# Gates, second shift and second scale as rows on four column tiles, carried to columns through DRAM

## The chip, the cores and the metric

The kernel runs on one core of one Trainium2 chip. The metric is the device time of one execution in microseconds, the median over runs. TensorE (PE in the profile; its weight loads are PEld), VectorE (DVE), ScalarE (ACT) and GpSimd (POOL) compute, and SyncE (SP) issues nearly all DMAs here. Each engine works through its own list of instructions in order.

## The reference

One transformer block on x of 2048 rows and 448 columns (S, D), in bf16, with six modulation vectors made from a row c:

```
mod = silu(c) @ w_mod                      # 448 -> 6 x 448
sa, ca, ga, sb, cb, gb = the six vectors of 448
h = layernorm(x) * (1 + ca) + sa
x = x + ga * A(h)                          # A: attention, 16 heads of 28, causal, window 256, then @ wo
h = layernorm(x) * (1 + cb) + sb
x = x + gb * B(h)                          # B: gated MLP with a spatial matmul
B(h): z = gelu(h @ w_in)                   # 448 -> 1792
      z1 = z[:, :896];  z2 = layernorm(z[:, 896:])
      g = w_sp @ z2 + b_sp                 # w_sp is 2048 x 2048
      return (z1 * g) @ w_out              # 896 -> 448
```

sa and sb are shifts, ca and cb scales, ga and gb gates.

## The kernel before, in words

**Tiles.** The 2048 rows are 16 tiles of 128 (NT) in four blocks of 512 (NB4). D is cut into four chunks of the contraction (DC; the last chunk has 64 rows of real data and is padded). An activation is kept transposed as hT, features on partitions and rows on the free axis, whenever it feeds a matmul as an operand over features.

**Order of the work.** Every instruction, or small group of them, is registered with `add` as an operation with its dependencies, the engines it may go to, and a duration for each. A planner has written a string ORDER (L19 to L75): one word `number.engine.slots` for each operation in the order of emission. `Sched.order` walks the string, puts every operation at the end of its engine's list and takes buffers by the slots; `count`, `waits` and `emit` then put in the semaphores. The durations and the constants beside them (HOP, NEXT, PEL, the `lat` and `tail` of a DMA) only feed the planner; what the program does is set by ORDER and the dependencies. An engine that waits holds everything behind it in its list.

**Stages, as the profile shows them.** Up to about 15 us: loads, the first modulation (t_mA, L554 to L564, in columns on PE), layer norm of the first block, its transposes on PE (L708), and warm matmuls on the identity (L578) that fill PE. About 15 to 110 us: projections to q, k, v (L756, L798, L840) and attention. A unit is a tile j of queries and half of the heads: scores on PE (L968, four row tiles of 32; L977 for some of the blocks, through QBD, which q_load copies from qT with four DMAs, L666), exponentials on ACT (L929), masks on DVE (L984), P times V on PE (L1011), then reciprocal and scaling on DVE (L1025, L1027). A DMA transpose (L476) turns o_sb into hT, PE multiplies by wo_g (L1035) and DVE adds to x (L1040). The second layer norm follows (`stats` L618, `norm` L638: DVE, POOL or ACT, L641 to L650), a DMA transpose, and the second modulation on hT (L1058 on ACT or L1060 on DVE or POOL). About 108 to 154 us: the two halves of w_in (L1097, L1143) with gelu on ACT, layer norm of z2 on POOL and DVE, ended by L1112 on POOL. From 154 us: 28 groups of 16 spatial matmuls (L1166), each of which depends on all z2 tiles, an addition on DVE (L1170), the product with z1 on POOL (L1173), the output projection (L1185), the residual on DVE (L1195) and the output DMA (L1200).

**The lines around the change.** After t_mA come, with scale and shift of the second modulation as columns, t_mB: 32 matmuls of one column each (L544, made by `mod_cols`), copied to modT by two DVE operations (`mod_out`, L569 and L570; the second adds 1), and a small DMA (d_modB, L589) that moves 64 partitions of modT up. t_gate (L591) makes the gates ga and gb as rows, broadcast on 64 partitions each: the stationary operand is sc_rep, silu(c) repeated in 64 columns, so that two column tiles hold the two gates. t_graw (L595) copies PSUM to gg_sb, and three DMAs (`spread`, L601) make both gates stand on all 128 partitions. POOL multiplies wo by ga (t_wog, L605, four operations) and w_out by gb (L1051, seven).

Of the kernel before, what the change touches and what calls it, by code (L numbers as in the profile page):

```python
# [9 lines left out]
HOP = 0.12  # L10

NEXT = {"dve": 0.08, "act": 0.11, "pool": 0.045}
# [11 lines left out]
187.p 188.p 189.p 193.p 179.p 192.p 181.a 182.a 150.v 151.v.2 197.v 157.a.3 183.a 167.p.5 164.p.6 191.p 218.p.3 190.p 168.v 169.a 195.a 165.v 166.v
194.v 200.p.7 226.v 230.v 227.v 219.a 180.a 196.a 204.a 201.p.5 198.p.6 202.v 232.v 231.v 228.v 229.v 233.v 53.v 205.a 199.p.1 203.a 378.p.0 209.p.0
220.p.7 224.p.6 206.p.1 379.a.0 384.p.0 225.a 44.g 51.g 213.v 52.v 43.g 234.g 235.g 210.a 385.a.1 207.p.0 211.a 221.a 380.v 382.v 236.v 239.g.0
237.v.1 113.p.1 238.v.2 115.v 240.v.3 114.v 403.p.0 117.p.0 388.v 118.v 244.p.1 208.p.6 404.a.2 405.a 212.a 245.v 386.v 241.p.0 410.p.0 222.p.7
381.p.0 383.p 214.s 217.s 216.s 215.s 17.s 24.s 20.s 18.s 22.s 120.s 119.s 21.s 19.s 246.a 242.v 243.v 411.a.3 249.p.1 223.a 412.a 250.a 247.p.0 248.a
430.p.0 432.p.0 387.p 389.p 431.a.4.0 275.v 279.v 281.v 277.v 282.v 280.v 278.v 276.v 283.g 326.v 284.g 390.v 391.v.0 285.v 332.v 413.v 406.v 408.v
287.v.0 415.v 434.v 288.g.1 292.s 291.s 253.p.1 261.p.0 254.a 438.p.0 262.a 439.a.5.1 265.p.1 407.p.0 259.p.0 409.p 266.a 260.a 459.p.0 460.a.6.2  # L30
433.a 251.p.1 414.p 267.p.0 416.p 467.p.0 468.a.0.3 328.v 289.v.2 293.s 286.v.3 330.v 252.v 435.v 290.s 268.v 417.v 418.v.1 329.v 263.p.1 440.p.0
273.p.0 441.a 264.a 257.s 256.s 121.s 258.s 255.s 392.s 419.s 436.p.0 488.p.0 464.v 333.v 327.v 331.v 442.v 443.v 489.a.1.4 437.p 444.p 271.p.1
461.p.0 445.p 463.v 334.g 471.v 274.v 446.v 447.v.2 272.v 462.a 296.a 294.g 297.g 295.g 335.g 496.p.0 497.a.2.0 269.p.0 469.p.0 465.p.0 466.p 298.p.1
470.a 517.p.0 299.a 270.v 336.v 493.v 500.v 490.p.0 300.p.0 473.p 316.p.1 472.v 492.v 301.v 518.a.3.1 521.v 317.v 491.a 525.p.0 498.p.0 474.p
526.a.4.2 475.v 476.v.0 530.v 340.v.0 529.v 501.v 522.v 124.g 337.g.1 125.g 339.g.2 122.g 338.g.3 123.g 448.s 341.s 343.s 342.s 477.s 344.s 318.p.0
312.p.1 494.p.0 319.a 313.a 499.a 546.p.0 302.p.0 519.p.0 495.p 420.p.1 502.p 547.a.5.3 554.p.0 520.a 555.a.6.4 303.v 551.v 421.v 503.p 527.p.0
304.p.0 310.p.1 504.v 505.v.1 559.v 558.v 422.v 305.a 528.a 575.p.0 576.a.0.0 393.p.0 548.p.0 523.p.0 524.p 531.p 532.p 583.p.0 394.v 550.v 345.v
533.v 580.v 534.v.2 549.a 311.a 584.a.1.1 314.p.0 315.v 478.p.1 556.p.0 552.p.0 479.v 346.v 116.s 306.s 506.s 309.s 307.s 535.s 308.s 557.a 604.p.0
449.p.0 553.p 560.p 561.p 577.p.0 605.a.2.2 578.a 612.p.0 613.a.3.3 423.v 588.v 587.v 579.v 450.v 562.v 507.p.1 585.p.0 480.v 395.v 563.v.0 508.v
347.g 348.g 324.p.0 581.p.0 325.a 586.a 633.p.0 634.a.4.4 351.p.1 606.p.0 320.p.0 582.p 607.a 321.a 641.p.0 642.a.5.0 608.v 509.v 609.v 396.v 451.v  # L40
452.v 481.v 397.g 453.g 398.g 482.g 454.g 510.v 617.v 424.v 352.v 589.p 590.p 614.p.0 591.v 536.p.0 616.v 322.p.1 537.v 592.v.1 646.v 511.v 399.v
637.v 400.v.0 401.g 455.g 425.g 615.a 323.a 662.p.0 663.a.6.1 355.p.0 610.p.0 635.p.0 611.p 618.p 619.p 636.a 356.v 670.p.0 671.a.0.2 538.v 620.v
638.v 621.v.2 349.p.1 643.p.0 353.p.0 639.p.0 644.a 350.a 691.p.0 564.s 402.s 666.v 645.v 675.v 622.s 593.s 692.a.1.3 664.p.0 640.p 647.p 648.p
361.p.1 699.p.0 456.v.1 354.v 649.v 667.v 539.v 358.s 359.s 360.s 23.s 357.s 665.a 565.p.0 672.p.0 426.g 483.g 427.g.2 540.g 541.g 362.a 365.p.1
700.a.2.4 650.v.0 457.v 696.v 668.p.0 674.v 566.v 366.v 567.v 673.a 720.p.0 721.a.3.0 669.p 363.p.0 676.p 693.p.0 677.p 594.p.1 694.a 701.p.0 702.a
728.p.0 729.a.4.1 704.v 703.v 364.v 678.v 695.v 679.v.2 595.v 623.p.0 725.v 624.v 568.v 724.v 596.v 722.p.0 697.p.0 373.p.1 723.a 749.p.0 698.p 705.p
369.p.0 706.p 730.p.0 750.a.5.2 370.a 731.a 757.p.0 569.v 733.v 374.v 484.g 485.g.0 486.g 512.g 651.s 458.s 487.s 680.s 860.s 570.g 428.g 513.g 429.s
514.g.1 597.v 625.v 598.g 515.g 707.v 571.v 708.v.1 709.s 758.a.6.3 367.p.1 751.p.0 726.p.0 727.p 368.a 752.a 626.v 732.v 734.p 735.p 753.v 754.v
736.v 737.v.0 761.v 778.p.0 779.a.0.4 371.p.0 652.p.1 759.p.0 755.p.0 762.v 653.v 782.v 783.v 654.v 372.a 760.a 786.p.0 756.p 763.p 780.p.0 764.p
787.a.1.0 375.p.1 681.p.0 781.a 788.p.0 376.a 789.a 807.p.0 765.v 655.v 766.v.2 790.v 791.v 682.v 656.v 683.v 843.v 844.v 784.p.0 785.p 792.p 793.p  # L50
809.p.0 710.p.1 808.a.2.1 810.a 815.p.0 572.g.0 542.g 794.v 795.v.1 811.v 812.v 573.g 627.g 599.g 845.g 600.g 543.g.2 544.g 846.g 628.g 574.s 601.g.0
516.s 738.s 545.s 602.g 657.g 739.p.0 817.p.0 813.p.0 814.p 658.v 629.v 630.g.1 631.g 711.v 816.a.3.2 892.p.0 893.p.1 818.a 659.v.2 819.v 820.v 767.s
603.s 850.a 848.a 847.a 821.p 822.p 768.p.1 377.s 796.s 632.s 684.v 712.v 660.v 661.s 849.v 823.v 713.v 824.v.0 685.v 740.v 769.v 686.g 687.g 714.g
715.g 894.p 895.p 927.p.2 928.p.3 929.p 930.p 896.a 904.a 910.p.0 911.p.1 825.s 688.v.0 689.v 770.v 741.v 771.v 690.s 716.v 717.v.1 718.g 905.g 772.g
773.g 939.a 742.v 774.v 940.v 775.v.2 797.p.0 798.v 799.v 800.v 743.g 776.g 744.g 931.a 941.a.0 826.p.1 942.g 745.g 746.g.0 747.g 827.v 801.v 898.v
# [212 lines left out]
def bass_adaLN_cond__sliding_block__mixer_gmlp__prompt_kernel(  # L268
# [1000 lines left out]
```

## Time and profile before

| what | us |
|---|---|
| median of three runs | 276.64 |
| lowest and highest run | 275.81, 276.93 |
| profiled execution | 277.14 |
| its span, first to last instruction | 275.2 |
| PE busy in the span | 264.7 |
| DVE, ACT, POOL busy | 159.3, 138.2, 117.6 |

The granted clock of TensorE is 0.999 over the span. In the profile a line of a group reads: line of the kernel, engine, operation, output and inputs with their shapes, xcount, then the busy time in us and the mean of one in ns, then the idle time of the engine just before them and what ended it. A window reads: start and end, length, then the busy time and count of PE, PEld, DVE, ACT and POOL, the granted clock, the DMA share and GB/s. A piece of the chain reads: start, length, engine and line. Mean durations of matmuls overlap, as they are pipelined: 32 of 163 ns each are busy for 0.9 us together.

### The profile page before, as it was taken

The page shows a single profiled execution, that of the slowest core. Times are in us where ns is not written, and L with a number is a line of the kernel's source. Part 1 is how long each engine was busy: PE and PEld are TensorE (multiplying, and loading weights), DVE is VectorE, ACT ScalarE, POOL GpSimd, SP SyncE. Part 2 cuts the span into 40 slices and gives each one's busy share as a digit, 9 for nine tenths or more (in the row PEclk, how much of TensorE's full clock was granted, in tenths as well). Part 3 has the DMA queues.
Part 4 walks back from the last instruction along what each step waited for, and adds up shares of the span by engine and source line. Part 5 has one row for each costly group of instructions (what it writes and reads, how often), then busy time and mean ns, then how long its engine had stood idle before and what let it go on. Part 6 is the DMA issues. An engine that isn't in the chain of part 4 may idle for free.

```text
span 275.2 us, 7464 instructions
## 1 busy us (share of the span) xinstructions
PE 264.7 (96%) x3221; PEld 143.6 (52%) x3246; DVE 159.3 (58%) x370; ACT 138.2 (50%) x189; POOL 117.6 (43%) x172
## 2 busy tenths in 40 slices
PE   5999999899999999999999999999999999999995
PEld 1766565566676866445444444444444444444552
DVE  5599999999999999779365202100331042233343
ACT  5689999899998999889998400000000000000000
POOL 8531229720364694364799105000853053425110
PEclk9999999999999999999999999999999999999999
DMA  7958953551156746937999999100000000002022
GB/s 204 288 190 202 306 104 74 68 77 37 21 61 114 111 67 103 172 60 114 175 196 187 187 198 204 44 0 0 2 0 0 0 2 0 0 0 86 16 92 76
DMA packets 66386, 26.41 MB, mean 96 GB/s; under 512 B 56881, under 2 KB 65266, under 8 KB 66354
## 3 DMA queue, kind: packets, MB, share of 16 engines
q1 hardware_dynamic: 66080, 25.48, 46.7%
q8 instruction: 25, 0.41, 0.6%
q10 hardware_dynamic: 274, 0.46, 0.5%
q14 instruction: 7, 0.06, 0.1%
HBM read 9.07 MB, written 1.84 MB: 40 GB/s over the span
## 4 chain that ended last, share of the span: by engine, by line
PE 77%; DVE 9%; POOL 4%; DMA 4%; issue 2%; SPq 2%; ACT 2%; POOLq 0%
PE ps L1166 35%; PE ps L1097 8%; PE ps L1185 8%; PE ps L1143 8%; PE ps L1011 4%; PE ps L1035 3%; PE ps L968 3%; DVE PT L984 2%; DMA x_sb<-in_A_x_dram 2%; PE ps L756 2%; PE ps L840 2%; POOL xn L646 2%; DMA wmod<-in_w_mod_dram 2%; POOL wo_g L605 1%; DVE st_all L621 1%
## 5 line engine op out<-in xcount | busy, mean ns | idle before, releaser
L929 ACT ACTIVATE PW<-ps 128x2048 bf16<-128x2048 f32 (+1 forms) x56 | 67.5, 1260 | 4.1 <-PE ps L968 3.4
L1173 POOL TENSOR_TENSOR z1T<-tmpg,z1T 128x512 bf16<-128x512 bf16 x28 | 31.8, 1152 | 77.8 <-DVE tmpg L1170 77.8
L1170 DVE TENSOR_TENSOR tmpg<-ps,bsp_bc 128x512 bf16<-128x512 f32 x28 | 19.1, 690 | 73.9 <-PE ps L1166 48.7
L1166 PE MATMUL ps<-wspB,z 128*128 128x512 bf16 x217 | 49.0, 379 | 0.4
L1166 PE MATMUL ps<-wspA,z 128*128 128x512 bf16 x220 | 48.3, 379 | 0.3 <-issue 0.2
L984 DVE TENSOR_TENSOR PT<-PW,mask 128x1024 bf16<-128x1024 bf16 x56 | 38.7, 723 | 0.1
L1166 PEld LDWEIGHTS ps<-wspA,z 128*128 128x128 bf16 x224 | 21.8, 98 | 26.6 <-issue 0.4
L1166 PEld LDWEIGHTS ps<-wspB,z 128*128 128x128 bf16 x224 | 21.9, 98 | 26.1
L1011 PEld LDWEIGHTS ps<-Vaug,PT 128*128 128x128 bf16 x496 | 22.3, 96 | 4.4 <-DVE o_sb L1027 0.5
L1011 PE MATMUL ps<-Vaug,PT 128*128 128x32 bf16 x496 | 24.4, 177 | 0.1
L629 POOL TENSOR_TENSOR rs_all<-ve_all,neghalf 128x1 f32<-128x1 f32 (+1 forms) x31 | 20.0, 650 | 9.3 <-DVE ve_all L626 8.7
L1185 PE MATMUL ps<-w_out_g,z1T 128*128 128x448 bf16 (+1 forms) x119 | 22.3, 341 | 0.0
L1097 PE MATMUL ps<-w_in,hT 64*128 64x448 bf16 x224 | 22.2, 349 | 0.1
L1143 PE MATMUL ps<-hT,w_in 64*128 64x512 bf16 x196 | 21.8, 376 | 0.0
L1011 PE MATMUL ps<-Vaug,PW 128*128 128x32 bf16 x224 | 20.4, 176 | 0.0
L1195 DVE TENSOR_TENSOR fin<-ps,x_sb 128x448 bf16<-128x448 f32 (+1 forms) x17 | 9.8, 593 | 17.2 <-PE ps L1185 17.2
L621 DVE BATCH_NORM_STATS2 st_all<-x_sb 128x6 f32<-128x448 bf16 x32 | 19.1, 613 | 0.5 <-DMA x_sb<-in_A_x_dram 0.5
L798 PE MATMUL ps<-hT,WQK 128*128 128x512 bf16 x66 | 17.2, 379 | 2.1 <-DVE rec_all L1025 0.7
L1011 PEld LDWEIGHTS ps<-Vaug,PW 128*128 128x128 bf16 x224 | 17.6, 96 | 2.4
L626 POOL TENSOR_SCALAR ve_all<-mv_all 128x1 f32<-128x1 f32 (+1 forms) x16 | 4.8, 297 | 31.5 <-DVE mv_all L624 30.9
L1185 PEld LDWEIGHTS ps<-w_out_g,z1T 128*128 128x128 bf16 x119 | 11.6, 98 | 10.0
L1151 ACT ACTIVATE z1T<-ps 128x512 bf16<-128x512 f32 x28 | 14.5, 608 | 4.2 <-PE ps L1143 4.0
(125 smaller groups left out, 370.6 us busy)
## 6 DMA issues: line engine op xcount, KB each, us to landing
out_dram<-fin SPq DMA_DIRECT2D x15, 112.0 KB, 1.7
x_sb<-in_A_x_dram SPq DMA_DIRECT2D x3, 448.0 KB, 5.8
wmod<-in_w_mod_dram SPq DMA_DIRECT2D x1, 1344.0 KB, 9.0
w_in<-in_B_w_in_dram SPq DMA_DIRECT2D x1, 1344.0 KB, 7.7
QBD<-qT SPq DMA_DIRECT2D x16, 64.0 KB, 2.2
w_out_g<-in_B_w_out_dram SPq DMA_DIRECT2D x1, 784.0 KB, 5.8
bsp_bc<-in_B_b_sp_dram SPq DMA_DIRECT2D x1, 512.0 KB, 4.6
x_sb<-in_A_x_dram SPq DMA_DIRECT2D x2, 224.0 KB, 3.9
```

Of the source, the lines that this page charges most:

```text
L621: st = [dve(0.62 if True else 0, lambda e, t=t, ci=ci, s=s: e.bn_stats(st_all[:, slot, t, ci, :], s()), deps(t), prio) for ci, s in enumer ...
L629: rs = pool(0.41 + 0.155 * len(tiles), lambda e: e.tensor_tensor(rs_all[:, slot, a:b], ve_all[:, slot, a:b], neghalf[:, 0:b - a], ALU.pow) ...
L798: m = pe(4 * MMS, [lambda e, h=h, g=g, kc=kc, tb=tb: e.matmul(ps[:, h.slot[0], :], lhsT=WQK[:, kc, 4 * g:4 * g + 4, :].rearrange("p a b -> ...
L929: ex = act(xdur, lambda e, out_ap=out_ap, in_ap=in_ap: e.activation(out_ap(), in_ap(), ACT.Exp, scale=SCALE), [s], v - 8.0 + u, takes, tab ...
L984: return dve(0.70, lambda e: e.tensor_tensor(cols(hp.slot[0] * 2048 + 1024 * k, [[256, 4], [128, 2], [1, 128]]), cols(at_w() + 128 + 192 * ...
L1011: fns.append(lambda e, hp=hp, hO=hO, hi=hi, bi=bi, kb=kb, hd=hd, nb=nb, a=at[hi][bi], p_of=p_of: e.matmul(ps[:, hO.slot[0], 32 * hd:32 * h ...
L1097: return lambda e, kc, p0, start, stop: e.matmul(ps[:, hs[t % 2].slot[hf], 0:D], lhsT=hT[p0:p0 + 64, kc, t * 128:(t + 1) * 128], rhs=w_in[ ...
L1143: return lambda e, kc, p0, start, stop: e.matmul(ps[:, hs[b // 2].slot[b % 2], :], lhsT=w_in[p0:p0 + 64, kc, ft * 128:(ft + 1) * 128], rhs ...
L1166: m = pe(16 * MMS, [lambda e, h=h, si=si, ft=ft, tb=tb: e.matmul(ps[:, h.slot[0], :], lhsT=z2[:, si, ft * 128:(ft + 1) * 128], rhs=(wspA i ...
L1170: a = dve(0.7, lambda e, h=h, ht=ht, tb=tb: e.tensor_tensor(tmpg[:, ht.slot[0], :], ps[:, h.slot[0], :], bsp_bc[:, tb * 512:(tb + 1) * 512 ...
L1173: u = pool(1.16, lambda e, ht=ht, ft=ft, tb=tb: e.tensor_tensor(z1T[tb][:, ft, :], tmpg[:, ht.slot[0], :], z1T[tb][:, ft, :], ALU.mult), [ ...
L1185: return [lambda e, ft=ft: e.matmul(ps[:, h.slot[0], c0:c1], lhsT=z1T[t // 4][:, ft, (t % 4) * 128:(t % 4 + 1) * 128], rhs=w_out_g[:, ft, ...
```

## The change

t_mB, `mod_cols` and the DMA d_modB are taken out. The gate group makes four vectors: ga, gb, sb and cb (v = 2, 5, 3, 4), each as a row repeated on 32 partitions, with sc_rep of 32 columns and four column tiles. One copy takes the bank to gg_sb. Four DMAs write one row each to a DRAM tensor `mod_rows`; two DMAs read the gates back, broadcast to 128 partitions; four read sb and cb back as columns of modT, one element of 4 bytes at a time; one operation adds 1 to the scale.

```diff
-    sc_rep, _, r_bytes = alloc("sc_rep", [128, DC, 64], BF16)
+    sc_rep, _, r_bytes = alloc("sc_rep", [128, DC, 32], BF16)
...
+    rows_d = nc.dram_tensor("mod_rows", (4, D), F32).ap()
...
-    hB = Hold(bM)
-    t_mB = pe(1.05, mod_cols(hB, (3, 4), False), [t_wmB, t_sc, t_p2], -15.0, [hB])
-    t_modB = mod_out(hB, 8, t_mB, -15.0)
-    dsem.append("d_modB")
-    t_modB.append(add({"sp": (0.6, lambda e: e.dma_start(modT[64:128, 11:13], modT[0:64, 11:13]))}, list(t_modB), -14.9, dma="d_modB", lat=0.05, tail=2.0))
     hG = Hold(bM)
     t_gate = pe(0.78, [lambda e, kc=kc, v=v, p0=p0: e.matmul(
-        ps[p0:p0 + 64, hG.slot[0], 0:D], lhsT=sc_rep[:, kc, :], rhs=wmod[:, kc, v * D:(v + 1) * D],
-        start=(kc == 0), stop=(kc == DC - 1), tile_position=(0, p0)) for kc in range(DC) for v, p0 in ((2, 0), (5, 64))],
-                [t_wmB, t_screp, t_p2], -14.0, [hG], "cols64")
-    t_graw = dve(0.7, lambda e: e.tensor_copy(gg_sb[:, 0, :], ps[:, hG.slot[0], 0:D]), [t_gate], -14.0)
+        ps[p0:p0 + 32, hG.slot[0], 0:D], lhsT=sc_rep[:, kc, :], rhs=wmod[:, kc, v * D:(v + 1) * D],
+        start=(kc == 0), stop=(kc == DC - 1), tile_position=(0, p0)) for kc in range(DC) for v, p0 in ((2, 0), (5, 32), (3, 64), (4, 96))],
+                [t_wmB, t_screp, t_p2], -14.0, [hG], "cols32")
+    t_graw = either(0.6, lambda e: e.activation(gg_sb[:, 1, :], ps[:, hG.slot[0], 0:D], ACT.Copy),
+                    0.62, lambda e: e.tensor_copy(gg_sb[:, 1, :], ps[:, hG.slot[0], 0:D]), [t_gate], -14.0)
     hG.until.append(t_graw)
-    t_gup = [spread("d_gg%d" % k, lambda p=p: gg_sb[p:p + 64, 1, :], lambda: gg_sb[64:128, 0, :], [t_graw]) for k, p in enumerate((0, 64))]
-    t_gg = [[t_graw, spread("d_gg2", lambda: gg_sb[64:128, 0, :], lambda: gg_sb[0:64, 0, :], [t_graw, t_gup])], t_gup]
+    t_rows = [small("d_row%d" % k, lambda k=k: rows_d[k:k + 1, :], lambda k=k: gg_sb[32 * k:32 * k + 1, 1, :], [t_graw]) for k in range(4)]
+    t_gg = [small("d_gg%d" % k, lambda k=k: gg_sb[:, k, :], lambda k=k: rows_d[k, :].partition_broadcast(128), [t_rows]) for k in range(2)]
+    t_modB = [small("d_mod%d" % k, lambda k=k: modT[:, (8, 13)[k]:(11, 16)[k]],
+                    lambda k=k: rows_d[2 + k, 0:384].rearrange("(c p) -> p c", p=128), [t_rows]) for k in range(2)]
+    t_modB += [small("d_mod%d" % (2 + k), lambda k=k: modT[64 * k:64 * k + 64, 11:13],
+                     lambda: rows_d[2:4, 384:448].rearrange("v p -> p v"), [t_rows]) for k in range(2)]
+    plus = lambda e: e.tensor_scalar(modT[:, 12:16], modT[:, 12:16], 1.0, None, ALU.add)
+    t_modB.append(add({"dve": (0.14, plus), "pool": (0.2, plus)}, list(t_modB), -13.9))
...
-            for c0, c1 in ((0, D // 2), (D // 2, D)) if t == NT - 1 else ((0, D),):
+            for c0, c1 in ((0, D // 2), (D // 2, 3 * D // 4), (3 * D // 4, D)) if t == NT - 1 else ((0, D),):
...
-                m = pe(k * one_mm, outs_of(range(k)), [us[:k], t_woutg], v + 0.01 * (c0 > 0), [h])
+                m = pe(k * one_mm, outs_of(range(k)), [us[:k], t_woutg] + (others if t == NT - 1 else []), v + 0.0001 * c0, [h])
...
```

`small` is `spread` with another tail for the planner. Three more things change with it.

- The durations and constants of the planner are set anew (HOP 0.12 to 0.055, PEL 0.2 to 0.34, OTAIL 4.0 to 2.8 and some twenty durations). They act on the program only through ORDER.
- ORDER is written anew as a whole. What it moves: 11 warm matmuls (L578) instead of 10; on SP the second x load ahead of wv, and the 64-row parts of two weights ahead of their other parts; on DVE the columns of the first modulation ahead of the padding copies; four of the second layer norm's products (L646) from DVE or ACT to POOL; three of the second modulation's products (L1058) from ACT to DVE and POOL; the first L1035 at a later place on PE; two early transposes of w_sp on SP instead of one, and b_sp ahead of the second half of w_sp. In all ACT's list goes from 172 to 168 operations, DVE's from 370 to 364 and POOL's from 168 to 178.
- The last tile (t = 15) is put out in three pieces of 224, 112 and 112 columns instead of two of 224, and they depend on the other tiles of the last block, so they come last.

More of the change, by code (lines that the diff above doesn't have):

```diff
@@ L24 @@
[L24 to L31, printed above, removed]
@@ L420, in bass_adaLN_cond__sliding_block__mixer_gmlp__prompt_kernel @@
     LO, HI, BOTH = slice(0, D), slice(D, 2 * D), slice(0, 2 * D)
-    t_c = load("d_c", "act", 0.01, lambda e: e.dma_start(c_row[:], c[0:1, :]), prio=-98.98, land=2.9)
-    t_wmA = [head("d_wmAa", "act", wmod, w_mod, 0, 2, BOTH, -98.97, 5.8, least=5.0), head("d_wmAb", "sp", wmod, w_mod, 2, 1, BOTH, -98.97, 4.3, least=3.6),
-             head("d_wmAc", "sp", wmod, w_mod, 3, 64, BOTH, -98.96, 5.3, least=3.8)]
+    t_c = load("d_c", "act", 0.01, lambda e: e.dma_start(c_row[:], c[0:1, :]), prio=-98.98, land=1.6, least=1.5)
+    t_wmA = [head("d_wmAa", "act", wmod, w_mod, 0, 2, BOTH, -98.97, 5.0, least=4.2), head("d_wmAb", "sp", wmod, w_mod, 2, 1, BOTH, -98.97, 4.1, least=3.4),
+             head("d_wmAc", "sp", wmod, w_mod, 3, 64, BOTH, -98.96, 5.5, least=3.8)]
     t_wq = []
-    for k, (n, cols, at) in enumerate((("q", LO, (6.2, 7.0, 7.2)), ("k", HI, (8.4, 9.1, 9.4)))):
+    for k, (n, cols, at) in enumerate((("q", LO, (5.8, 6.6, 6.8)), ("k", HI, (8.1, 8.9, 9.1)))):
         a, b, c_ = [head("d_w%s%s" % (n, p), "sp", wq_st, A_wqkv, first, rows, cols, -98.95 + 0.03 * k + 0.004 * i, at[i], (), 3.9)
@@ L480, in pe @@
     def pe(dur, fns, deps=(), prio=0.0, take=(), shape="full"):
-        op = add({"pe": (dur, fns)}, deps, prio, take, lat=PEL)
+        op = add({"pe": (dur, fns)}, deps, prio, take, lat=0.2 if shape == "rows32" else PEL)
         op.shape = shape
@@ L533, in bass_adaLN_cond__sliding_block__mixer_gmlp__prompt_kernel @@
     t_qz = [[clear(b, q) for q in range(2)] for b in range(2)]
-    t_screp = dve(0.5, lambda e: e.tensor_copy(sc_rep[:], sc_sb[:].unsqueeze(2).broadcast_to([128, DC, 64])), [t_sc, t_x[1]], -16.0)
-    def mod_cols(h, vs, bank_col):
-        fns = []
-        for vi, v in enumerate(vs):
-            for ch in range(DC):
-                m = 128 if ch < 3 or not bank_col else 64
-                for kc in range(DC):
-                    fns.append(lambda e, v=v, ch=ch, kc=kc, m=m, col=vi * 4 + (ch + (vi and vs[0] > 0)) % 4: e.matmul(
-                        ps[0:m, h.slot[0], col:col + 1], lhsT=wmod[:, kc, v * D + ch * 128:v * D + ch * 128 + m],
-                        rhs=sc_sb[:, kc:kc + 1], start=(kc == 0), stop=(kc == DC - 1)))
-                if ch == 3 and bank_col:
-                    for kc in range(DC):
-                        fns.append(lambda e, v=v, kc=kc, col=vi * 4 + 3: e.matmul(
-                            ps[64:128, h.slot[0], col:col + 1], lhsT=wmod[:, kc, v * D + 384:v * D + 448],
-                            rhs=sc_sb[:, kc:kc + 1], start=(kc == 0), stop=(kc == DC - 1), tile_position=(0, 64)))
-        return fns
+    t_screp = dve(0.5, lambda e: e.tensor_copy(sc_rep[:], sc_sb[:].unsqueeze(2).broadcast_to([128, DC, 32])), [t_sc, t_x[1]], -16.0)
     hA = Hold(bM)
@@ L1031, in bass_adaLN_cond__sliding_block__mixer_gmlp__prompt_kernel @@
         done = [[QK_ready[(g, j // 4)] for g in range(4)], [K_ready[(g, 4 * (j // 4) + i)] for g in range(4) for i in ((j % 4,) if j // 4 in FINE else range(4))], [V_ready[j]]]
-        oe = turn("d_oT%d" % j, lambda j=j: hT[:, :, j * 128:(j + 1) * 128], lambda ho=ho: o_sb[:, ho.slot[0], :], [t_o, done], v - 9.0, tail=3.2 if j == NT - 1 else OTAIL)
+        oe = turn("d_oT%d" % j, lambda j=j: hT[:, :, j * 128:(j + 1) * 128], lambda ho=ho: o_sb[:, ho.slot[0], :], [t_o, done], v - 9.0, tail=2.0 if j == NT - 1 else OTAIL)
         ho.until.append(oe)
@@ L1039, in bass_adaLN_cond__sliding_block__mixer_gmlp__prompt_kernel @@
         mo_of[j] = mo
-        t_x1 = dve(0.62, lambda e, h=h, j=j: e.tensor_tensor(x_sb[:, j, :], ps[:, h.slot[0], 0:D], x_sb[:, j, :], ALU.add), [mo], v - 8.0 + DEFER)
+        t_x1 = dve(0.61, lambda e, h=h, j=j: e.tensor_tensor(x_sb[:, j, :], ps[:, h.slot[0], 0:D], x_sb[:, j, :], ALU.add), [mo], v - 8.0 + DEFER)
         h.until.append(t_x1)
@@ L1190, in bass_adaLN_cond__sliding_block__mixer_gmlp__prompt_kernel @@
                 k = 6 if tb == NB4 - 1 else 7
[L1191 removed]
+                m = pe(k * one_mm, outs_of(range(k)), [us[:k], t_woutg] + (others if t == NT - 1 else []), v + 0.0001 * c0, [h])
                 if k < 7:
[L1193 removed]
+                    m = pe(one_mm, outs_of([6]), [us, m], v + 0.02 + 0.0001 * c0)
                 hf = Hold(fiR)
+                others.append(m)
                 f = dve(0.15 + (c1 - c0) / 950.0, lambda e, h=h, hf=hf, t=t, c0=c0, c1=c1: e.tensor_tensor(
[L1196 removed]
+                    fin[:, hf.slot[0], c0:c1], ps[:, h.slot[0], c0:c1], x_sb[:, t, c0:c1], ALU.add), [m, all_C], v + 0.0001 * c0, [hf])
                 h.until.append(f)
```

160 lines of the change are left out of this document (83 added, 77 removed).

## The prediction

> **What bounds the kernel now.** I read the page first: the busy shares, then the slices.
>
> ```profile
> PE 264.7 (96%) x3221; PEld 143.6 (52%) x3246; DVE 159.3 (58%) x370; ACT 138.2 (50%) x189; POOL 117.6 (43%) x172
> ...
> PE   5999999899999999999999999999999999999995
> DVE  5599999999999999779365202100331042233343
> ACT  5689999899998999889998400000000000000000
> POOL 8531229720364694364799105000853053425110
> ```
>
> TensorE is busy 96% of the span, so hardly any idle time is left to win: 275.2 - 264.7 = 10.5 us, and the wait for the first weights is over half of it. But the mean hides stages. In slices 3 to 16 (about 14 to 110 us) DVE, ACT and PE all show nines at once; from slice 23 on PE stands alone. The table by stage shows which of them has room.
>
> ```profile
> 5.00:15.00 10.00, 9.38 (x88) 6.51 (x89) 5.12 (x21) 5.84 (x12) 6.36 (x13) 1.00 1.02 296
> 15.00:30.00 15.00, 14.69 (x217) 9.18 (x217) 13.94 (x40) 14.54 (x25) 3.87 (x7) 1.00 0.72 191
> 30.00:45.00 15.00, 14.48 (x353) 9.02 (x361) 14.44 (x33) 14.78 (x17) 6.27 (x7) 1.00 0.80 168
> 45.00:55.00 10.00, 8.62 (x191) 5.21 (x195) 9.97 (x16) 8.42 (x10) 8.52 (x7) 1.00 0.42 60
> 55.00:80.00 25.00, 24.25 (x637) 15.95 (x637) 24.67 (x55) 23.63 (x24) 7.83 (x13) 1.00 0.26 46
> 80.00:105.00 25.00, 24.99 (x694) 18.49 (x694) 24.83 (x54) 23.80 (x25) 16.18 (x27) 1.00 0.64 97
> 110.00:135.00 25.00, 25.00 (x262) 12.38 (x260) 17.86 (x59) 21.90 (x39) 12.32 (x31) 1.00 0.82 133
> 135.00:150.00 15.00, 15.00 (x144) 6.75 (x140) 8.54 (x27) 13.76 (x26) 14.27 (x25) 1.00 1.06 177
> 155.00:270.00 115.00, 114.48 (x544) 54.00 (x553) 27.15 (x43) 1.99 (x5) 33.67 (x30) 1.00 0.20 45
> ```
>
> The columns are stage and length, then busy time of PE, PEld, DVE, ACT, POOL. From 45 to 55 DVE has no gap (9.97 of 10) while PE loses 1.38. From 80 on PE is full with DVE just beneath it (24.83 of 25). POOL has gaps of 12.7 from 110 to 135 and runs at 14.27 of 15 from 135 to 150. From 155 on only PE counts. The granted clock is 1.00 throughout. The chain of waits says who ended last.
>
> ```profile
> 9.53 0.85 PE ps L578 x2
> ...
> 17.77 0.39 ACT qT L783
> ...
> 22.75 6.13 DMA x_sb<-in_A_x_dram
> ...
> 52.21 1.44 POOL wo_g L605
> 53.70 0.93 PE ps L1035 x4
> ...
> 153.91 0.16 issue
> ...
> 261.97 9.95 PE ps L1185 x56
> 271.95 0.62 DVE fin L1195
> ```
>
> The columns are start, length and piece. Up to 53.7 the chain runs through DMA, DVE and POOL: the last x load is issued at 22.75, behind the first block's QBD copies, DVE's statistics follow it, and at 53.70 PE's first output projection (L1035) waits for the fourth wo_g product on POOL. Later it is mostly PE.
>
> The profiled execution took 277.14 us for a span of 275.2, so 1.94 lie around the span; it is 0.50 above the median of 276.64. I sum the change against the execution and take it off the median.
>
> **The change part by part.** *The columns on PE go.*
>
> ```profile
> L544 PE MATMUL ps<-sc_sb,wmod 128*128 128x1 bf16 x32 | 0.9, 163 | 0.0
> L591 PE MATMUL ps<-wmod,sc_rep 128*64 128x448 bf16 x8 | 0.9, 359 | 0.0
> L595 DVE COPY gg_sb<-ps 128x448 f32<-128x448 f32 x1 | 0.6, 625 | 0.2 <-PE ps L591 0.2
> L646 POOL TENSOR_SCALAR xn<-x_sb,rs_all,ve_all 128x448 bf16<-128x448 bf16 x13 | 14.3, 1103 | 4.5 <-DVE ve_all L633 4.1
> L1060 POOL TENSOR_SCALAR hT<-hT,modT 128x512 bf16<-128x512 bf16 x3 | 3.0, 997 | 2.0 <-DMA hT<-xn 2.0
> ```
>
> 32 matmuls of one column keep PE for 0.9 us, and they go: **-0.9**. In their place the gate group has 16 matmuls of 448 columns instead of eight. Before, eight in pairs took 0.9 us, or 0.22 a pair, where one alone in L1185 takes 9.95 / 56 = 0.18: a pair runs together. If four on 32-column tiles run together, the new group costs 4 x 0.22 = 0.9 again; one after another it would be 16 x 0.18 = 2.9, so +2.0. I take 0, being nearest to the L591 row, and keep +2.0. The copy out of PSUM (0.6) stays as one copy. Two small copies on DVE go and a "plus 1" on four columns comes; all are a few tenths.
>
> *The trip through DRAM.* SP issues ten small DMAs where it had four.
>
> ```profile
> gg_sb<-gg_sb SPq DMA_DIRECT2D x3, 112.0 KB, 6.1
> modT<-modT SPq DMA_DIRECT2D x1, 0.5 KB, 2.9
> 39.24 0.53 SPq L601 DMA_DIRECT2D gg_sb<-gg_sb  x1
> ```
>
> Six more issues at 0.53 are 3.2 us of SP, whose waits elsewhere are long. No row shows a DRAM round trip of this kind; these bound one leg at 2.9 to 6.1 us, two legs at 6 to 12. The four row DMAs follow the last x load, so they cannot delay it; behind them queue the rest of wo_g, w_in and the xn transposes. The first broadcast stands behind four transposes and one QBD copy, at about the 39.24 where the old third copy stood, and lands as that did, before the wo_g products; its wait for the rows holds the QBD copies behind it only if a row takes over ten us. The column DMAs stand behind the transposes of o_sb of tile 6, at about 70, the last at about 75. With 6.1 us the last lands near 81; the "plus 1" on DVE comes at about 101 by the work ahead of it. So 0, covered by 20 us; uncovered it would be 6 to 12 us. It couldn't gain, since nothing on the chain waited for the old ones.
>
> *Order, head.* One more warm matmul stands ahead (an L578 pair is 0.85, so at most +0.43, and only where PE isn't waiting). The x load of the second block moves ahead of wv on SP, and the columns of the first modulation are written on DVE ahead of the padding copies. Summing DVE's durations in the new order, the first block's last normalised tiles come about 1.5 us earlier, while ACT's work ahead of the first exponential is 0.65 less. The first q copy at 17.77 releases the last x load, so what the head gains goes down the whole chain of DMA and DVE. Ends +0.2 and -1.0; I take **-0.6**, what ACT allows.
>
> *Order, middle.* The first L1035 stands later on PE, where its four wo_g products will be done. The stretch from 45 to 55 loses 1.38 there; of it I take back **-0.5**, the rest being DVE's. With before's durations put in the new order, the work ahead of the last scores falls from 92.7 to 91.3 us on PE, from 89.0 to 87.7 on ACT, and ahead of the last mask from 92.0 to 90.3 on DVE; 0.55 of PE's reappears later. All three shrink together, so none newly bounds the stage. POOL grows: L646 there goes from 13 to 17, L1060 from 3 to 5, one hT product leaves: 4 x 1.10 + 2 x 1.00 - 1.0 = +5.4.
>
> *Tail.* The last tile ends in three pieces, two of them on DVE after PE's end. Two of about 0.2 and 0.28 with one more DMA issue come to what one piece and its issue took before: 0, within 0.1 either way.
>
> **Sum:** -0.9 - 0.6 - 0.5 = -2.0; 277.14 becomes 275.1, the median **274.6**.
>
> **The rivals.** *More POOL work slows DVE.*
>
> ```profile
> 45.00:55.00 10.00, 7.66 (x9) 1.00 0.42 60
> 55.00:80.00 25.00, 11.38 (x18) 1.00 0.26 46
> ```
>
> These are the masks alone (L984 on DVE): 0.85 us each where POOL is 85% busy, 0.63 where it is 31% busy. That is 9 x 0.22 = 2.0 us of DVE for 8.5 of POOL, 0.23 per us. Of the 5.4, some 3.5 lie ahead of the last scores: +0.8 at this rate, +3.5 if every microsecond were lost. In the middle, +1.7, it leaves -0.3: 276.3, no change; at its end +1.5, 278.1. Against it stands DVE's own -1.7. The Trainium skill, SBUF — State Buffer, section "Who interferes with whom", has the two share a port pair under an exclusive lock, where the second to start waits the whole operation out. By that rule it would be the +3.5, 278.1; the masks' 0.22 show it in part.
>
> *POOL ends late for the spatial matmuls: the slower side.*
>
> ```profile
> 135.19 1.04 POOL L1051 TENSOR_TENSOR w_out_g<-w_out_g,gg_sb 128x448 bf16<-128x448 bf16 x1
> 149.90 2.54 POOL L1112 TENSOR_SCALAR z<-z,rs_all,ve_all 128x896 bf16<-128x896 bf16 x2
> ```
>
> Before, POOL ended z at 152.44, 1.47 before PE asked at 153.91; the first L1166 waits for every z tile. From the same L1051 to the last z the new order has 17.7 us of POOL work against 17.2, and 4.6 us more stand ahead of it, into the 12.7 us of gaps between 110 and 135. If it starts no later than 135.2 it ends by 152.9, and PE asks at about 152: most of the gain stays. If the gaps don't take the extra work, say a start at 138.0, it ends at 155.7, 1.8 after 153.91: 278.4. It decides from a start of 136.2. For it: POOL is in order, nearly full, and most of its work there waits on ACT and DVE. Against: the gaps are over twice what is added.
>
> *The new order removes more idle.* PE loses 3.6 us between 5 and 80 (the five rows above). If all but 0.5 went, with -0.9: 272.6.
>
> *The change does not do what it says:* the four tiles run one after another, +2.0, all gain gone: 276.6. Against: L591's pairs, and the L968 scores on four row tiles.
>
> **How the numbers follow.** Forecast 0.42, more idle removed 0.13, DVE slowed 0.17, POOL late 0.20, tiles in sequence 0.08. What a measurement of this kernel can tell is 0.5%, 1.4 us: below 275.26 is faster, above 278.02 slower. Faster has the forecast but for its upper end (0.40) and the more-idle case: 0.53. Slower has the late POOL and a little of the slowed DVE: 0.22. The rest, 0.25, is the same. Low end 272.3, just past the more-idle case; high end 278.5, to hold the late POOL at its price. The forecast's own range is 273.6 to 275.8.
>
> **What would show it.** Right: no L544; a gate group of about 0.9 us with PE's next work behind it; the first L1035 without a wait for wo_g; the last mask on DVE 1 to 2 us earlier; the last row of columns landed well before its "plus 1"; L1166 begun near 152 without waiting for POOL; span about 273.2. Wrong: masks beside POOL work at 0.85 over a longer stretch, a wait of PE for L1060 or L1112 of POOL, or a gate group of 3 us.

## The result, and the profile after

The changed kernel took 278.64 us (median of 6 runs, 277.81 to 279.06) against 276.63 for the kernel before (6 runs): the ratio is 1.007, 95% interval 1.0047 to 1.0092. In a second set of runs it took 278.36 (12 runs) against 277.05 (35 runs), ratio 1.0035, interval 1.0017 to 1.0054. So it is slower by some 0.35 to 0.7%, which is 1.0 to 1.9 us (1.3 to 2.0 by the medians; a ratio is estimated from all runs of a set and need not be the quotient of two medians). The forecast was 274.6, with a range of 272.3 to 278.5.

The profiled execution took 277.81 for a span of 276.1; it is the shortest of the first six runs, so it does not show what lengthens the others. Here is the page after: the busy shares, then the table by stage in the same columns as before.

```profile
PE 265.1 (96%) x3230; PEld 142.0 (51%) x3230; DVE 161.2 (58%) x364; ACT 134.8 (49%) x185; POOL 124.2 (45%) x182
```

```profile
5.00:15.00 10.00, 7.06 (x87) 5.03 (x86) 8.29 (x24) 5.35 (x11) 7.13 (x13) 1.00 1.09 310
15.00:30.00 15.00, 14.90 (x223) 8.97 (x227) 13.09 (x38) 14.52 (x25) 3.77 (x7) 1.00 0.58 176
...
45.00:55.00 10.00, 9.88 (x219) 5.75 (x216) 9.91 (x17) 8.81 (x10) 7.55 (x7) 1.00 0.36 63
55.00:80.00 25.00, 25.00 (x603) 15.94 (x601) 22.58 (x48) 24.27 (x26) 6.95 (x10) 1.00 0.41 70
80.00:105.00 25.00, 24.04 (x718) 17.48 (x706) 24.50 (x55) 23.75 (x23) 18.34 (x29) 1.00 0.50 83
...
135.00:150.00 15.00, 15.00 (x146) 7.03 (x144) 9.45 (x25) 14.25 (x28) 11.64 (x22) 1.00 1.13 195
```

From 45 to 80 PE is fuller than before (9.88 and 25.00, where it had 8.62 and 24.25). The first output projection, which had waited 0.42 for wo_g, now has no wait; that is a third of what the stretch from 45 to 55 gains. But DVE idles 2.4 us from 55 to 80, mostly waiting for PE, and from 80 to 105 PE loses 0.96 where it had lost 0.01; 0.7 of that are waits for DVE. What the order won early it gave back in part when DVE became the bound. The chain of waits shows what comes after.

```profile
138.38 15.13 PE ps L1127 x140
153.53 0.60 ACT z1T L1135
154.12 0.49 ACTq L1202
154.61 0.50 ACT z1T L1135
155.16 69.23 PE ps L1151 x320
...
258.63 14.62 PE ps L1170 x91
273.27 0.28 DVE fin L1181
```

(Lines have moved: L1166 is now L1151, L1143 is L1127, L1112 is L1096, L1185 is L1170.) PE is done with w_in at 153.53, 0.4 us earlier than before, but the first spatial matmul starts at 155.16, 1.1 us later. The chain names ACT's z1T copies. The first L1151 does not depend on those at 154.61; its bank's last user had been copied by 151.8. What it does depend on is all of z2, and the timeline of POOL and DVE shows this arrive last:

```profile
132.46 1.04 POOL L1035 TENSOR_TENSOR w_out_g<-w_out_g,gg_sb 128x448 bf16<-128x448 bf16 x1
...
133.85 1.06 POOL L1117 TENSOR_TENSOR rs_all<-ve_all,neghalf 128x1 f32<-128x1 f32 x2
137.42 0.74 POOL L613 TENSOR_TENSOR rs_all<-ve_all,neghalf 128x1 f32<-128x1 f32 x1 [2.50 <-DVE ve_all L610]
...
141.95 1.04 POOL L1035 TENSOR_TENSOR w_out_g<-w_out_g,gg_sb 128x448 bf16<-128x448 bf16 x1
...
144.17 1.03 POOL L1035 TENSOR_TENSOR w_out_g<-w_out_g,gg_sb 128x448 bf16<-128x448 bf16 x1
...
153.57 1.09 POOL L1096 TENSOR_SCALAR z<-z,rs_all,ve_all 128x896 bf16<-128x896 bf16 x1
...
153.61 1.29 DVE L1118 TENSOR_SCALAR z<-z,mv_all,rs_all 128x896 bf16<-128x896 bf16 x1 [1.73 <-POOL rs_all L1117]
155.13 1.85 PEld L1151 LDWEIGHTS ps<-wspA,z 128*128 128x128 bf16 x10 [2.14 <-POOL z L1096]
```

The brackets give the idle time before an instruction and what ended it. POOL waits until 137.42 for a DVE operation; from there its list is full for 17.2 us, to 154.66. DVE's last z product, which needs a POOL result, ends at 154.90, and PE starts right after it. This product takes 1.29 us beside POOL's last one; the median of the eight of its kind is 0.51.

### The profile page after: what moved, and what is told of

Read it like the earlier page. It is cut to its first block, busy times and chain, and to the rows that moved or that the text cites. A ratio compares the mean times of both kernels' runs of the same rounds, so it can differ in the third digit from the quotient of the medians.

```text
span 276.1 us, 7474 instructions
## 1 busy us (share of the span) xinstructions
PE 265.1 (96%) x3230; PEld 142.0 (51%) x3230; DVE 161.2 (58%) x364; ACT 134.8 (49%) x185; POOL 124.2 (45%) x182
## 4 chain that ended last, share of the span: by engine, by line
PE 77%; DVE 15%; ACT 2%; DMA 2%; issue 1%; POOL 1%; ACTq 0%; DVEq 0%
PE ps L1151 35%; PE ps L1081 8%; PE ps L1127 8%; PE ps L1170 8%; DVE PT L968 6%; PE ps L782 5%; PE ps L995 3%; PE ps L824 3%; PE ps L1019 3%; PE ps L952 2%; DMA wmod<-in_w_mod_dram 2%; DVE o_sb L1011 1%; DVE st_all L605 1%; DVE x_sb L1024 1%; POOL rs_all L613 1%
## 5 line engine op out<-in xcount | busy, mean ns | idle before, releaser
L1151 PE MATMUL ps<-wspA,z 128*128 128x512 bf16 x224 | 48.5, 380 | 1.7 <-ACT z1T L1135 1.7
L1151 PE MATMUL ps<-wspB,z 128*128 128x512 bf16 x224 | 49.2, 380 | 0.0
L968 DVE TENSOR_TENSOR PT<-PW,mask 128x1024 bf16<-128x1024 bf16 x56 | 37.9, 708 | 0.2 <-ACT PW L913 0.2
L1151 PEld LDWEIGHTS ps<-wspA,z 128*128 128x128 bf16 x224 | 21.8, 98 | 28.4 <-POOL z L1096 2.1
L1151 PEld LDWEIGHTS ps<-wspB,z 128*128 128x128 bf16 x224 | 21.9, 98 | 26.3
L613 POOL TENSOR_TENSOR rs_all<-ve_all,neghalf 128x1 f32<-128x1 f32 (+1 forms) x31 | 21.8, 710 | 14.3 <-DVE ve_all L610 13.2
L995 PEld LDWEIGHTS ps<-Vaug,PT 128*128 128x128 bf16 x496 | 21.5, 96 | 4.3 <-DVE PT L968 1.0
L1127 PE MATMUL ps<-hT,w_in 64*128 64x512 bf16 x196 | 22.1, 377 | 0.0
L1170 PE MATMUL ps<-w_out_g,z1T 128*128 128x448 bf16 (+2 forms) x126 | 22.0, 332 | 0.0
L782 PE MATMUL ps<-hT,WQK 128*128 128x512 bf16 x80 | 19.6, 380 | 0.1
L995 PEld LDWEIGHTS ps<-Vaug,PW 128*128 128x128 bf16 x224 | 17.7, 96 | 1.9
L1170 PEld LDWEIGHTS ps<-w_out_g,z1T 128*128 128x128 bf16 x126 | 11.7, 98 | 10.1
L630 POOL TENSOR_SCALAR xn<-x_sb,rs_all,ve_all 128x448 bf16<-128x448 bf16 x17 | 16.0, 944 | 1.1 <-DVE ve_all L617 0.5
L1081 PEld LDWEIGHTS ps<-w_in,hT 64*128 64x128 bf16 x224 | 10.8, 94 | 10.5 <-DVE mv_all L1108 0.3
```

Source lines behind the costliest of these rows:

```text
L613: rs = pool(0.41 + 0.155 * len(tiles), lambda e: e.tensor_tensor(rs_all[:, slot, a:b], ve_all[:, slot, a:b], neghalf[:, 0:b - a], ALU.pow) ...
L782: m = pe(4 * MMS, [lambda e, h=h, g=g, kc=kc, tb=tb: e.matmul(ps[:, h.slot[0], :], lhsT=WQK[:, kc, 4 * g:4 * g + 4, :].rearrange("p a b -> ...
L968: return dve(0.68, lambda e: e.tensor_tensor(cols(hp.slot[0] * 2048 + 1024 * k, [[256, 4], [128, 2], [1, 128]]), cols(at_w() + 128 + 192 * ...
L995: fns.append(lambda e, hp=hp, hO=hO, hi=hi, bi=bi, kb=kb, hd=hd, nb=nb, a=at[hi][bi], p_of=p_of: e.matmul(ps[:, hO.slot[0], 32 * hd:32 * h ...
L1081: return lambda e, kc, p0, start, stop: e.matmul(ps[:, hs[t % 2].slot[hf], 0:D], lhsT=hT[p0:p0 + 64, kc, t * 128:(t + 1) * 128], rhs=w_in[ ...
L1127: return lambda e, kc, p0, start, stop: e.matmul(ps[:, hs[b // 2].slot[b % 2], :], lhsT=w_in[p0:p0 + 64, kc, ft * 128:(ft + 1) * 128], rhs ...
```

## The experiments

Theory 1: the new order costs the time, by ending z2 late on POOL. Theory 2: the gates, the column tiles or the trip through DRAM cost it. Each kernel was timed beside the kernel before, in four sets on four chips. Ratios to it are given, since its own median lay between 276.8 and 277.2 in the four sets; kernels of different sets compare best by their ratios.

**The changed kernel again (after_again).**

> The changed kernel itself, once more, for its times beside the others and a second profile. Median 278.3 to 279.0 by both theories. Theory 1 (POOL ends z2 late and every L1151 waits for all of z2): PE stands idle 1.0 to 2.7 us ahead of the first L1151, and the longer of its executions differ in this wait or in what leads up to it. Theory 2 (the trip through DRAM or the four column tiles cost the time): the idle time lies elsewhere, before 100 us.

278.36, ratio 1.0035. Its profile took 279.02, and from the first scores on it is 0.9 to 1.4 us later than the first one: L926 starts at 17.89 instead of 16.95, L1151 at 156.55 instead of 155.16, after a wait of 1.90. So beside the wait for z2 something in the head differs between executions. TensorE's granted clock in this head (the column after POOL):

```profile
10.00:12.00 2.00, 0.67 (x6) 0.31 (x4) 1.86 (x6) 0.94 (x4) 1.99 (x5) 1.00 1.15 314
12.00:14.00 2.00, 1.40 (x11) 1.02 (x12) 1.96 (x4) 1.01 (x2) 1.29 (x2) 0.67 0.99 321
14.00:16.00 2.00, 2.00 (x11) 1.39 (x10) 1.30 (x3) 0.29 (x2) 0.00 (x0) 0.50 0.94 367
```

PE has little to do from 10 to 12 us, and then the clock falls to a half until 16. The 28 matmuls ahead of the first scores show what that cost here, the first profile's row ahead of this one's:

```profile
13.78 3.23 PE L740 MATMUL ps<-hT,WQK 128*128 128x256 bf16 x28 [0.40 <-DVE WQK L596]
13.48 4.48 PE L740 MATMUL ps<-hT,WQK 128*128 128x256 bf16 x28
```

That is 1.25 us more in this execution, the longest of its twelve. It is not what sets the median: the mean granted clock is 0.994 here and 0.999 or 1.000 in the other eleven, whose median is 278.35.

**z2 ahead of the w_out_g products (z_first).** In POOL's list, as the string ORDER has it:

```diff
- ... 976.g 842.g 942.g 846.g 999.g ... 1017.g 1012.g
+ ... 976.g 942.g 999.g ... 1017.g 1012.g 842.g 846.g
```

> The changed kernel, with two w_out_g products (L1035, 1.04 us each on POOL, at 141.95 and 144.17) moved behind the last z2 product in POOL's list. Theory 1 (POOL ends z2 late): POOL ends 2.1 us earlier, at about 152.6; PE is then ready at 153.5, its wait of 1.6 us goes, and the time falls by 1.3 to 1.6 us, to about 277.1. Theory 2 (gates and DRAM cost it): no change, 278.3 to 278.9. Theory 3 (the wait is for ACT's z1T copies, which the chain names): no change either, with PE still starting L1151 at about 155.1.

276.72, ratio 0.9977 (0.9957 to 0.9997), 1.64 us below the changed kernel of the same set. Its timeline shows the wait gone:

```profile
152.23 1.09 POOL L1096 TENSOR_SCALAR z<-z,rs_all,ve_all 128x896 bf16<-128x896 bf16 x1
152.28 1.29 DVE L1118 TENSOR_SCALAR z<-z,mv_all,rs_all 128x896 bf16<-128x896 bf16 x1 [1.73 <-POOL rs_all L1117]
153.29 2.17 POOL L1035 TENSOR_TENSOR w_out_g<-w_out_g,gg_sb 128x448 bf16<-128x448 bf16 x2
...
154.32 1.89 PE L1151 MATMUL ps<-wspA,z 128*128 128x512 bf16 x8 [0.16 <-issue]
```

z is whole at 153.57, PE's bracket is down to 0.16, and this in an execution whose head was a late one. ACT's copies go on beside it (from 154.20), so theory 3 falls.

**The new gates in the old order (gates_alone, gates_early).** The old ORDER with the new gate operations in the places of the old ones, and the old tail; in the second kernel the addition of 1 stands earlier on DVE:

```diff
- 654.v 125.v        (gates_alone: the "plus 1" at 100.4 us)
+ 541.v 125.v        (gates_early: at about 73 us)
```

> The changed gates (four column tiles, rows to DRAM and back) in the old order: before's list with the old operations' places taken by the new ones, and the old tail of two pieces. Theory 1 (the new order costs it, the gates don't): 32 matmuls (0.9 us) less on PE, some of it hidden: 275.7 to 276.5, not above before. Theory 2 (the gates and the DRAM trip cost it): 277.5 to 279.

> The gates alone in the old order once more, with the addition of 1 to the scale columns moved on DVE from 100.4 us to about 73 (the columns had landed at 60.3), so that the first second-modulation product on POOL (which waited 3.34 us for it) doesn't wait. Theory 1 (the gates cost nothing by themselves, my place for the addition cost 0.5 to 0.9 behind 107 us): 276.7 to 277.1, level with before. Theory 2 (ten small DMAs and the trip through DRAM cost it): 277.4 to 277.8 as without this edit. If the 32 matmuls less were worth their 0.9 us on PE: 276.1.

277.60 (1.0018, interval 0.9999 to 1.0037) and 276.63 (0.9985, interval 0.9966 to 1.0003). By its median the first lies in theory 2's range, but its profile names another cause: my place for the addition held up a POOL product by 3.34 us. With it moved, the gates are level with before or a little better. They do not cost the time. Nor is a gain of 0.9 shown: where the 32 matmuls had stood, PE now waits for ACT.

```profile
21.60 0.40 PE L926 MATMUL ps<-qT,KT 32*128 32x128 bf16 x16 [0.80 <-ACT PT L913]
21.93 0.94 PE L569 MATMUL ps<-wmod,sc_rep 128*32 128x448 bf16 x16
```

This is the timeline of gates_early. The sixteen matmuls on four column tiles take 0.94 together, as eight on two had.

**The new order with the old gates (order_alone).** ORDER and tail of the changed kernel, gates of the kernel before.

> The new order and the new tail of three pieces with the old gates (32 column matmuls, two column tiles, no DRAM). Theory 1 (the order costs it): the wait ahead of the first spatial matmul stays, and the 0.9 us of L544 comes back in part: 278.5 to 279.6. Theory 2 (the gates cost it): 275.5 to 276.8, below before or beside it.

278.99, ratio 1.0058 (1.0037 to 1.0079), 0.6 above the changed kernel; z ends on POOL at 155.75 in its profile (154.66 and 1.09). The order costs the time; the new gates take about 0.6 of it back, which is not clear of noise, as the two intervals overlap.

**The statistics back on DVE (stats_back).**

```diff
- 1031.g 944.g 976.g 1033.g 992.g 1009.g 1016.g
+ 1031.v 944.v 976.v 1033.v 992.v 1009.v 1016.v
```

> The changed kernel with seven small statistics operations of the last z2 and layer norm tiles (0.19 to 0.35 us each, 1.6 us together, at 140 to 153 us) put from POOL back to DVE, where the old order had them. Theory 1 (POOL's list is full from 137 us to the last z2, so any POOL work taken out there counts one for one, until PE's own arrival at 153.5): -1.2 to -1.6, 276.8 to 277.2, much as with the w_out_g products. Rival (POOL is late because of what it was given before 137, or because it starts on a wait): less than -0.5.

277.28, ratio 1.0000 (0.9978 to 1.0022): 1.1 below the changed kernel by the medians of two sets, 1.0 by the ratios, a little short of the 1.2 expected; the two intervals overlap a little. In its profile PE's bracket ahead of L1151 is 0.16 too. Two different things taken out of POOL's last stretch help alike, so it is the length of that list that counts.

**Warm matmuls in the head (warm_fill, z_first_warm).** Eight more ahead of the second pair of transposes, without and with the z2 edit:

```diff
+ 76.p.7 77.p.7 78.p.7 79.p.7 80.p.7 81.p.7 82.p.7 83.p.7
  171.p.7 168.p.4
```

> The changed kernel with eight more warm matmuls (L561, 0.22 us each, on one bank) on PE ahead of the second pair of transposes, where PE stood idle 1.8 us from 10.96 to 12.76. Theory 1 (in most executions the idle PE of the head drops TensorE's clock to 0.5 for about 3 us, as the second profile of the changed kernel shows at 12 to 16 us, and this costs 1.1 us behind it): the clock stays at 1.00 in the head, and the time falls by 0.5 to 1.1 us, to 277.2 to 277.9, and less spread. Theory 2 (the clock's drop is caught up by 30 us, since DVE and ACT set the pace there): no change, 278.2 to 278.6.

> Both edits: the two w_out_g products behind the last z2 product, and the eight warm matmuls. If both causes hold and add up: 276.72 less 0.5 to 1.1, so 275.6 to 276.2, below the kernel before (277.05 in the last runs). If the clock's drop does not matter: 276.5 to 276.9.

278.90 (1.0056, interval 1.0028 to 1.0083) and 277.18 (0.9999): no gain, and neither in the range that was expected. In the profile of warm_fill the clock stays at 1.00, but its eight matmuls stood on PE from 12.61 until the transposes at 14.35 and held these past 13.38, when DVE had been ready. In that of z_first_warm the clock is at 0.50 from 10 to 12 us all the same. So this does not tell what a filled head is worth. It did show what sets the transposes: DVE's L626 (L625 in the others) took 1.17 us there.

**The clears held (clear_later).** DVE's normalisation of the fourth tile takes 0.38 elsewhere. Here it is in the head of the changed kernel, and of stats_back, beside POOL:

```profile
11.54 1.17 DVE L625 TENSOR_SCALAR xn<-x_sb,mv_all,rs_all 128x448 bf16<-128x448 bf16 x1
12.63 1.10 DVE L596 COPY WQK<-wq_st 128x448 bf16<-128x448 bf16 x1
11.63 1.97 POOL L531 MEMSET QBD<- 128x1024 f32 x2
```

```profile
12.19 2.06 DVE L625 TENSOR_SCALAR xn<-x_sb,mv_all,rs_all 128x448 bf16<-128x448 bf16 x1
12.28 1.83 POOL L531 MEMSET QBD<- 128x1024 f32 x2
```

While POOL clears the second QBD buffer in two parts of 0.95, a DVE operation that takes 0.38 took 1.17, as if the first part were waited out, or 2.06, as if both were. Where it took 1.17, the copy behind it took 1.10 instead of 0.27, so DVE lost 1.6 to 1.7 us to the two parts either way. The Trainium skill, SBUF — State Buffer, section "Who interferes with whom", says that DVE in its two-port mode and GpSimd exclude each other for a whole instruction. These rows agree in that whole parts were waited out; but DVE's start is recorded 0.09 ahead of POOL's, so they do not show that the later one waits, and no run shows which mode L625 uses. The clears wait only for the second x load and their turn on POOL. That load now stands ahead of wv on SP. One line holds them:

```diff
+    for q in t_qz[1]:
+        q.deps.add(sc.ops[170])     # DVE's last hT chunk of the first block
     sc.order()
```

> The changed kernel, with POOL's two clears of the second QBD buffer (L531, 0.95 us each, which run at 11.6 to 13.6 us beside DVE's fourth normalisation) held until DVE has made the first block's last hT chunk (14.5 us); nothing else moves. Theory 1 (the clears hold DVE: its L625 took 1.17 us in one profile and 2.06 in two others where 13 of its kind take 0.38, so the second transposes start 0.8 to 1.7 us late, and all behind them): L625 takes 0.4, the first scores (L926) start at 16.0 to 16.9 instead of 16.9 to 18.0, and the time falls by 0.7 to 1.5 us, to 276.9 to 277.7, with the wait ahead of L1151 still there. Rival 1 (the head's delay is caught up in the middle): 278.2 to 278.6. Rival 2 (the head is held by the loads' landing, which differs from execution to execution): L625 shorter, but PE not earlier and the time unchanged.

277.36, ratio 1.0016 (0.9994 to 1.0037): 1.0 below the changed kernel by the medians of two sets, 0.5 by the ratios, whose intervals overlap. In its profile:

```profile
11.67 0.40 DVE L625 TENSOR_SCALAR xn<-x_sb,mv_all,rs_all 128x448 bf16<-128x448 bf16 x1
11.98 0.27 DVE L596 COPY WQK<-wq_st 128x448 bf16<-128x448 bf16 x1
```

The first scores start at 16.42, 0.5 earlier than in the first profile, and the wait ahead of L1151 is still there at 1.7 us: two separate causes. That the clears stretch DVE is shown; what they cost the whole kernel lies between 0.5 and 1.0 and is not clear of noise.

**All three edits (all_three), with the old gates (three_old_gates), with two pieces at the end (three_tail_two).**

> Three edits of the changed kernel together: the w_out_g products behind the last z2 product, the seven small statistics operations back on DVE, and the clears held. If z2's end (1.6 us) and the clears (0.7 to 1.5 us) are separate causes, they add up: 275.2 to 276.2, below before (277.0) by 0.8 to 1.8. If only z2 counts: 276.7, level with before.

275.95, ratio 0.9971 (0.9949 to 0.9993): the kernel is below before and below the changed one. Against z_first alone it gains 0.8 by the medians of two sets but only 0.2 by the ratios (0.9971 and 0.9977), so that the causes add up is not shown by these times.

> The three edits in the new order (all_three), but with the old gates: 32 one-column matmuls, two column tiles, no DRAM trip. Theory 1 (where PE is full the 0.9 us of the 32 matmuls count): 0.5 to 1.0 us above all_three, 276.5 to 277.0. Theory 2 (they fall into time in which PE waits for ACT or DVE anyway, as in the old order, where taking them out moved the rest of PE by nothing): 275.8 to 276.2, equal to all_three.

276.42, ratio 0.9983 (0.9959 to 1.0007). The difference to all_three, 0.12% or some 0.3 us, is within what the intervals leave open; 0.9 is not shown.

```diff
-            for c0, c1 in ((0, D // 2), (D // 2, 3 * D // 4), (3 * D // 4, D)) if t == NT - 1 else ((0, D),):
+            for c0, c1 in ((0, D // 2), (D // 2, D)) if t == NT - 1 else ((0, D),):
```

> The three edits (all_three), with the last tile put out in two pieces of 224 columns instead of 224, 112 and 112; the last tile still comes last. My forecast had the three pieces at 0 within 0.1 us: 275.8 to 276.1. The two profiles show 2.9 us from the last matmul to the end of the span with the new tail and 3.3 with the old one; if that is due to the third piece, this kernel is 0.2 to 0.4 us above all_three; if it is due to the last tile being forced to the end, it equals it.

275.18, ratio 0.9936 (0.9915 to 0.9957), the fastest kernel here and below all that was expected. The ends of the chains, all_three first:

```profile
256.65 14.62 PE ps L1170 x91
271.29 0.28 DVE fin L1181
```

```profile
255.68 14.60 PE ps L1170 x84
270.37 0.39 DVE fin L1181
```

Their spans are 274.1 and 272.8, so 2.83 us follow the last matmul with three pieces and 2.52 with two: the third piece costs 0.3. (The other profiles with three pieces have 2.8 to 2.9.) The rest between the two profiles is a head that was 1.0 us earlier: in all_three its chain of waits runs through an x load that landed at 9.63, in three_tail_two through a part of w_mod that landed at 6.74. How much of the difference of the medians is the tail's beyond 0.3 is open.

## Why the prediction was wrong

**The step that failed** is the one on POOL, under the slower rival: "If it starts no later than 135.2 it ends by 152.9, and PE asks at about 152: most of the gain stays." The product it counts from (the old L1051 at 135.19) ran at 132.46, earlier than the condition asked, and z still ended at 154.66, 22.2 us later where I had summed 17.7. Two things make up these 4.5 us. The list holds eight more operations than the old one (33 against 25, 18.2 us busy against 16.5), which with the gaps between them come to 19.7, 2.0 more than I had summed. And 2.50 us of it were a wait, which I had left out, since I had only asked when the list starts: POOL waited for DVE, which is in order too.

```profile
135.50 0.63 DVE L605 BATCH_NORM_STATS2 st_all<-z 128x6 f32<-128x448 bf16 x1 [2.43 <-ACT z L1092]
...
137.24 0.10 DVE L610 TENSOR_SCALAR ve_all<-mv_all 128x1 f32<-128x1 f32 x1
...
134.55 0.92 ACT L1092 ACTIVATE z<-ps 128x896 bf16<-128x896 f32 x1
```

A gap in an in-order list is no room for work if what ends it comes from elsewhere. Here a gelu on ACT at 134.55 held a DVE statistic, behind it the 0.10 us operation that POOL needed, and behind that 17 us of POOL. That the list's length counts was shown by z_first and stats_back; the wait at its start is read from the trace, and no run removed it. The rival had the right place, the right sign and nearly the right price (278.4; the median was 278.64, just past the range), but I gave it 0.20, with gaps upstream as the reason against it. That its price came so near is in part luck: it had z end at 155.7 and PE ask at 153.91, where the profile has 154.90 and 153.53, a wait of 1.6 and not 1.8, and the rest of the median came from elsewhere.

**The head, -0.6**, was right in the profile that was first seen (first scores at 16.95, before 17.66) and wrong in three others with this head (17.89 to 18.00 in after_again, z_first and stats_back). I had taken DVE's durations out of the old order, where nothing ran beside them. The second x load's earlier place let POOL's clears run into DVE; holding them was worth 0.5 to 1.0, within noise. In z_first and stats_back L625 took 2.06; in after_again it took 1.17 as in the first profile, and the clock's fall made the delay. Which of these lengthens the median is not shown.

**The 32 matmuls, -0.9**, were mis-sized: 0.3 to 0.6 by the pairs of runs, none of them clear of noise. In the old order PE waits for ACT where they had stood; for the new order no row shows the reason. That sixteen matmuls on four column tiles cost no more than eight on two was right (0.9 us).

**wo_g, -0.5**, was right (the wait of 0.42 is gone; 45 to 55 went from 8.62 to 9.88), but 0.96 was lost again from 80 to 105, with DVE as the bound. By the first scores PE was 0.7 ahead, by 153.53 only 0.4.

**The tail, 0**, came out better: from the last matmul to the end of the span 3.28 us before and 2.85 after (271.92 to 275.2, 273.25 to 276.1). It is the forced last place of the last tile, so that a small piece and not a whole tile follows PE's end; the third piece costs 0.3.

**Right were** the DRAM trip at 0, the gates as no cause, and that masks would not suffer. The columns were issued by 70.8 us, the addition ran at 101.20, and POOL did not wait for it. The first broadcast did come late, as I had not said: POOL waited 1.3 us for it ahead of the wo_g products, but PE did not. The masks:

```profile
45.00:55.00 10.00, 5.12 (x7) 1.00 0.36 63
55.00:80.00 25.00, 10.77 (x17) 1.00 0.41 70
```

In these rows of L968 alone a mask takes 0.73 and 0.63, not 0.85; over all 56 the median is 0.68, as before. The contention that I gave a rival for was there, but elsewhere: in the head, with a clear as its partner, and in DVE's last z product.

In sum, against the forecast of -2.0 for the profiled execution, whose span rose by 0.9: the arrival at the spatial matmuls gained 0.4, the wait ahead of them grew by 1.5 (0.16 to 1.63), the matmuls after it took 0.2 more (118.09 against 117.86), and the tail gave back 0.4. The median is 0.8 above that execution, and this part stays open: the second profile's later head is the clock's fall, which the other eleven executions of its set do not have.

## What to carry to other kernels

When a stage waits for all of something, look at the engine that ends it as a list: from its last wait to its end, count every operation, and put behind it what nobody needs yet. Idle time upstream on an engine that works in order is not slack unless you know what ends each gap. When a load is moved earlier, ask which operation it releases, and what that then runs beside.

## What the runs showed of the hardware

Beside two POOL clears of 0.95 us in a row, a DVE operation of 0.38 took 1.17 with the next one stretched as well, or 2.06. A DVE z product with a median of 0.51 took 1.29 beside POOL's z product of 1.09.

TensorE's granted clock fell to 0.50 for some 3 us after a stretch with 0.67 us of work in 2 (after_again); the first profile had a like gap (1.80 us of idle before the transposes), and stats_back one of 2.02, at a clock of 1.00 throughout. The Trainium skill, TensorE: Matmul & The Clock Gate, section "Part 1: The HAM clock gate", calls the window in which activity is judged free-running and its effect different from run to run; these profiles agree.

The first part of w_mod from ACT landed between 5.7 and 7.7 us in the eleven profiles with the new order. The head's chain of waits starts with a landing of w_mod in nine of them and with an x load, at 9.26 and 9.63, in the other two (z_first, all_three).
